# Gate and down weights on SyncE's queue behind the last token transpose, up weights on ScalarE's: a linear-attention and GEGLU block on one core

## The chip, the cores and the metric

The kernel runs on one core of a Trainium2 chip. The core has five engines that work side by side, each through its own list of instructions in order: TensorE (matmuls, PE in the profile), VectorE (DVE), ScalarE (ACT), GpSimd (POOL) and SyncE (SP), which here only issues DMAs. DMAs are issued on a queue of SyncE's or of ScalarE's, and the packets of both queues are moved by the same 16 DMA engines. The metric is the device time of one execution in microseconds (us); less is better.

## The reference

The block has two halves, both on x of 2048 tokens by 448 features, in bf16:

```python
h  = x + A(layernorm(x))          # linear attention, 16 heads of 28
h2 = h + B(layernorm(h))          # gated MLP, 448 -> 1792 -> 448

# A: q, k, v = split(x @ wqkv); phi(t) = where(t > 0, t + 1, exp(t)) + 1e-6
kv  = einsum("bhsd,bhse->bhde", phi(k), v)      # a sum over all tokens
z   = einsum("bhsd->bhd", phi(k))               # a sum over all tokens
o   = einsum("bhqd,bhde->bhqe", phi(q), kv) / (einsum("bhqd,bhd->bhq", phi(q), z) + 1e-6)
A   = o @ wo
# B:
B   = (gelu(x @ w_gate) * (x @ w_up)) @ w_down
```

So no token's attention output can be made before all tokens' keys have gone into kv and z. The gate and up weights are 448 x 1792 each (1.6 MB), the down weights 1792 x 448 (1.6 MB).

## The kernel before

The 2048 tokens are 16 tiles of 128. The work has three stages.

*Keys and queries.* For each tile, VectorE, ScalarE and GpSimd normalise the tokens (`ln_tile`, lines 430 to 455). The first four tiles are transposed by TensorE, the other twelve by DMA transposes on SyncE's queue (xT_4 to xT_15, line 455). TensorE then multiplies by the key or query weights (k_t and q_t, line 469), and adds phi(k) times the normalised tokens into four PSUM banks over all tiles (pt, line 488). ScalarE and VectorE make phi.

*The turn.* When the last key tile is in, kv is formed (line 527), masked by heads (kvm, line 531), and multiplied by wo into w2 (lines 547 to 553). Two DMAs on SyncE's queue, dws0 and dws1 (line 555), copy w2 into w2s with the two halves of the partitions exchanged. From here on the tiles go in pairs (`a2_pair`, line 558): the normalised queries of pair p are transposed, for pair 0 by TensorE (tro, line 599), for the others by a DMA on SyncE's queue (oT_1 to oT_7, line 605). The attention output of pair 0 is out1 (line 617), that of the other pairs is outA_p and outB_p (lines 627 and 628), which use pqnT, w2 and w2s and run two matmuls at once on the two halves of TensorE's rows. hr adds the residual (line 633), then come the second layernorm and its transposes: trh_0 and trh_1 on TensorE for pair 0 (line 654), and DMA transposes hT_2 to hT_15 on SyncE's queue (line 665), each behind a copy wrap_t on VectorE (line 664).

*The MLP.* The tokens go in chunks of 2, 2, 4, 4 and 4 tiles (`gu_chunk`, line 707). gu2_v and gu4_v (lines 726 and 728) multiply by gate weights on rows 0 to 63 and by up weights on rows 64 to 127 at the same time, so the gate weights lie in partitions 0 to 63 of wgu_sb and the up weights in partitions 64 to 127. ScalarE applies the GELU (ge, line 746) and VectorE the product (hm, line 748). downA_p and downB_p (line 696) multiply by wd_sb, fo adds the residual (line 702), and do_t stores the tile (line 703; the last two tiles, lines 678 to 683).

*The order.* Every task is numbered as it is created, and ORDERS (line 15) gives for each engine the full list of task numbers in the order in which it is to run them, in the order TensorE, ScalarE, VectorE, GpSimd, SyncE. `place` (line 130) checks that the lists agree with the dependencies, and `plan` (line 174) works out the semaphore waits. HOLD (line 51) says which of several waits of one task is put first. An engine that waits for one task holds up all that follows in its list. DMAs made by `dma` (line 345) keep their order of creation on a queue, through `last`.

The weights of the MLP are five loads: dwg0 and dwu0 (the first 768 of the 1792 columns of gate and up, 672 KB each), dwg1 and dwu1 (the other 1024, 896 KB each) and dwd (down, 1568 KB, 128 partitions). Before, the four gate and up loads stand on ScalarE's queue in the order dwg0, dwu0, dwg1, dwu1, created at lines 510 and 511 to run no earlier than ek_11, the exponential of key tile 11. dwd stands on ScalarE's queue too, created at line 609 with pair 1, and runs behind ge1_0, the first GELUs.

The order of the engines around the turn, before, by task names:

```text
SyncE:   ... xT_14 xT_15 dws0 dws1 oT_1 oT_2 oT_3 hT_2 hT_3 oT_4 hT_5 hT_4 hT_6 hT_7 oT_5 ...
ScalarE: ... ek_12 ek_13 dwg0 ek_14 dwu0 rq_4 ek_15 dwg1 eq_4 z1 eq_5 rq_5 dwu1 deA_0 ...
         ... ge0_0 ge1_0 deP_3 dwd ge1_1 ge0_1 ...
TensorE: ... out1_0 out1_1 q_11 q_12 q_13 q_15 q_14 outA_1 trh_0 trh_1 outB_1 gu2_0 gu2_1 outA_2
         gu2_2 outB_2 gu2_3 gu2_4 gu2_5 outA_3 gu2_6 outB_3 downA_0 gu2_7 gu2_8 downB_0 ...
```

Of the kernel before, what the change touches and what calls it, by code (L numbers as in the profile page):

```python
# [12 lines left out]


ORDERS = (
    "29 35 37 46 44 66 71 62 64 53 55 76 79 84 70 75 89 83 104 99 119 88 114 103 129 141 118 153 133 177 145 157"
    " 165 190 222 203 216 232 169 182 248 195 181 194 207 208 220 236 252 238 221 237 253 260 254 294 257 263 299"
    " 301 297 303 321 266 323 325 326 269 272 275 281 278 362 339 343 363 431 436 388 441 389 446 451 456 414 461"
    " 415 466 498 503 467 508 513 481 518 523 482 528 565 548 570 575 549 580 533 585 590 656 595 657 600 605 610"
    " 534 682 615 620 683 625 630 699 704 709 635 714 719 724 636 729 734 739 744 641 749 754 642 764 759 786 781"  # L20
    " 769 796 791 770 806 801 816 811 775 826 821 776 836 831 846 841 851 860 852 857 863",
    "3 5 6 7 28 32 33 41 42 36 59 60 45 50 51 67 54 72 63 94 77 95 80 109 110 78 124 85 125 136 137 91 90 148 172"
    " 149 100 173 185 106 186 115 105 160 130 161 142 211 243 198 199 154 120 212 244 178 227 121 228 166 191 204"
    " 217 284 233 285 224 249 286 223 288 239 240 287 314 292 291 261 256 262 318 353 259 357 255 302 298 322 324"
    " 258 268 264 265 271 270 267 333 335 334 336 277 384 283 279 282 276 340 274 273 280 345 432 434 410 361 439"
    " 437 444 442 449 447 452 454 457 459 462 477 464 501 499 506 504 544 509 511 516 514 519 521 524 526 529 531"
    " 568 566 571 573 652 578 581 576 583 678 586 588 593 591 598 596 601 603 613 608 611 606 616 618 623 621 628"
    " 626 631 633 700 702 712 707 705 710 715 717 720 725 727 722 730 732 737 735 747 745 742 740 757 750 752 755"
    " 767 765 760 762 787 784 782 789 794 797 799 792 807 809 802 804 812 817 814 819 822 829 824 827 839 837 834"
    " 832 849 847 842 844",  # L30
    "0 30 31 39 40 34 57 43 58 38 48 49 47 61 52 68 92 56 93 69 65 107 73 108 74 122 81 123 82 134 86 135 146 170"
    " 147 171 87 183 158 184 101 159 102 196 241 197 116 242 117 209 131 210 132 225 1 143 226 144 155 156 179 180"
    " 167 168 192 193 346 307 218 219 234 205 308 206 235 309 250 251 348 347 349 290 289 310 311 313 293 315 317"
    " 316 352 295 356 319 379 296 358 354 300 320 304 359 355 380 327 330 328 331 329 405 332 383 337 341 385 338"
    " 342 386 406 344 364 367 365 409 433 435 411 472 412 366 440 438 368 369 443 445 393 390 450 448 391 473 377"
    " 374 453 455 394 460 458 539 395 476 540 392 465 463 419 420 416 478 417 421 479 502 543 418 400 403 500 673"
    " 470 505 507 647 545 426 648 429 512 510 515 517 546 520 522 525 468 527 483 486 532 530 651 487 567 569 572"
    " 574 653 484 674 654 553 550 577 488 579 677 551 584 582 587 589 679 594 554 485 592 552 555 680 597 599 661"
    " 602 604 560 662 658 563 493 607 609 612 496 537 614 619 617 624 687 622 629 627 659 535 634 632 701 703 688"
    " 708 706 711 713 716 663 660 718 684 721 689 723 685 637 728 726 686 733 731 736 738 639 694 748 743 671 697"  # L40
    " 741 668 746 758 753 756 751 768 766 645 643 761 763 788 785 790 783 800 793 798 795 773 771 810 808 805 803"
    " 815 820 818 813 828 830 823 825 840 838 779 833 835 777 850 848 845 843 853 855 861 858 864",
    "15 16 27 19 22 21 17 96 97 111 25 112 126 127 138 139 150 151 26 23 174 162 187 175 200 188 163 245 201 18 213"
    " 214 229 20 230 24 246 312 350 351 381 382 407 408 370 371 372 373 376 474 475 397 541 398 396 542 402 399 422"
    " 423 424 425 428 649 650 676 675 490 491 489 557 558 556 492 562 559 495 664 665 691 666 692 667 690 693 696"
    " 670",
    "2 4 8 9 10 11 12 13 14 98 113 128 140 152 176 189 164 202 215 231 247 305 306 360 387 413 375 378 480 404 401"
    " 427 430 547 655 681 471 564 561 497 494 538 638 469 672 698 669 695 536 774 778 644 780 640 646 856 862 772"
    " 859 854 865",
)  # L50
HOLD = {
    32: (31,), 66: (36,), 99: (98,), 175: (174,), 188: (187,), 232: (231,), 294: (291,), 305: (298,), 362: (360,),
    388: (387,), 498: (378,), 767: (764,), 787: (786,), 807: (806,), 839: (836,), 864: (863,),
}


# [173 lines left out]
def bass_sequential_preLN__linear_attn_block__glu_gated_geglu__prompt_kernel(  # L230
# [19 lines left out]
    with es:  # L250
        block = es.enter_context(nc.Block())

        def sb(name, shape, dt):
            return es.enter_context(nc.sbuf_tensor(name, shape, dt))
# [7 lines left out]
        wgu_sb = sb("wgu_sb", [128, NK, FF], BF16)  # L262
        wd_sb = sb("wd_sb", [128, NJ, D], BF16)
# [41 lines left out]
        def bufs(name, n):  # L305
            return [_Buf("%s%d" % (name, i)) for i in range(n)]
# [7 lines left out]
        b_wo, b_wg, b_wu, b_wd = _Buf("wo"), bufs("wg", 2), bufs("wu", 2), _Buf("wd")  # L314
# [15 lines left out]
        A_, B_ = slice(0, 64), slice(64, 128)  # L330
# [14 lines left out]
        def dma(q, out_ap, in_ap, w, name, r=(), after=()):  # L345
            t_ = G.add(q, lambda e: e.dma_start(out_ap, in_ap), r=r, w=w, name=name, kind="dma", after=list(after) + last[q])
            last[q] = [t_]
            return t_

        def op(eng, fn, r, w, name, after=()):  # L350
            return G.add(eng, fn, r=r, w=w, name=name, after=after)
# [106 lines left out]
        eks = []  # L458
# [48 lines left out]
        xts = [t for t in G.all if t.name.startswith("xT_")]  # L507
        for i in range(2):
            cs = slice(0, FC) if i == 0 else slice(FC, FF)
            dma("act", wgu_sb[A_, :, cs], B_w_gate[:, cs].rearrange("(k p) n -> p k n", p=64), [b_wg[i]], "dwg%d" % i, after=eks[11:12])  # L510
            dma("act", wgu_sb[B_, :, cs], B_w_up[:, cs].rearrange("(k p) n -> p k n", p=64), [b_wu[i]], "dwu%d" % i, after=eks[11:12])


        op("act", lambda e: e.activation(zbc[B_, :], ps[B_, BK_PT[3], 0:D], AF.Identity), [b_ps[BK_PT[3]]], [b_z[1]], "z1")
        op("dve", lambda e: e.tensor_copy(zbc[A_, :], zbc[B_, :]), [b_z[1]], [b_z[0]], "z0")
# [42 lines left out]
        def a2_pair(p):  # L558
# [3 lines left out]
            if p < 2:  # L562
# [3 lines left out]
                for t in (a, a + 1):  # L566
                    n = t % 2
                    eng = "dve" if t in T1_DVE else "pool"
                    op(eng, lambda e, t=t, n=n: e.tensor_tensor(t1[:, n, :], pq[:, t, :], zbc[:, :], ALU.mult), [b_pq[t]] + b_z, [b_t1[n]], "t1%s_%d" % (eng[0], t))
                for t in (a, a + 1):  # L570
                    n, i = t % 2, t % 4
# [8 lines left out]
            else:  # L580
                i, b2 = 2 * (p % 2), slice(a, a + 2)
# [22 lines left out]
            else:  # L604
                G.add("sp", lambda e, i2=i2: e.dma_start_transpose(pqnT[:, i2, 0:NK, :], pqn[:, i2, 0:2 * D]),
                      r=b_pqn[i2], w=b_pqnT[i2], name="oT_%d" % p, kind="dma")

            if p == 1:
                dma("act", wd_sb[:, :, :], B_w_down.rearrange("(j p) n -> p j n", p=128), [b_wd], "dwd")

            if p == 0:
                for n in range(2):
# [139 lines left out]
        for nt in B1_CHUNKS:  # L752
            while done < min(P, (t0 + HR) // 2):
                a2_pair(done)
                done += 1
                if tbl2 is None:
                    tbl2 = G.add("act", lambda e: e.preload_act_table(AF.Gelu_apprx_tanh), name="tbl2", kind="nosync", after=exps)
            gu_chunk(t0, nt)
            for t in range(t0, t0 + nt, 2):
                if t < T - 2:  # L760
                    b2_pair(t // 2)
                else:
                    b2_tile(t)
                    b2_tile(t + 1)
            t0 += nt
# [52 lines left out]
```

## Time and profile before

| what | us |
|---|---|
| median of 3 runs | 191.95 |
| range of the runs | 191.61 to 192.84 |
| the profiled execution, its own time | 192.45 |
| its span, from the first to the last instruction | 190.7 |
| TensorE busy | 185.5 |
| VectorE busy | 127.7 |
| ScalarE busy | 76.0 |
| GpSimd busy | 52.3 |

The granted TensorE clock was 0.999. All times in the text below that name a place ("at 49.35") are microseconds from the start of the profiled span. The profile is one execution; the runs were timed without it. TensorE's busy time counts a stretch once, even if two matmuls run in it at the same time; the matmuls' ends are modelled, so the distance between the starts of two matmuls tells more of TensorE's speed than the length of one. A task of the kernel is found in the profile by its line, its engine and its place in the engine's order.

In a row of the profile, "L627 <- DMA pqnT<-pqn" reads: an instruction of line 627 waited for the DMA that writes the tile pqnT from the tile pqn. "SPq" and "ACTq" are the instructions of SyncE and ScalarE that issue DMAs; the time behind them is that of the issue, and the DMA lands later.

### The profile page before, as it was taken

To read this page: it belongs to the slowest core of one execution; us is meant where nothing else is said; L and a number is where in the kernel's file an instruction comes from. 1 tells how busy PE (TensorE), PEld (TensorE's weight loads), DVE (VectorE), ACT (ScalarE), POOL (GpSimd) and SP (SyncE) were. 2 spreads that over 40 slices of the span, in tenths; PEclk is the share of its full clock that TensorE was granted. 3 is DMA by queue.
4 is the path that set the end of the run, shared out by engine and by line. 5 is a ranking of instruction groups with operands and counts; after the bars stand their busy time and mean duration, and the time that the engine had idled before them with its cause. 6 is when DMAs were issued, how large, how long until landed. Compare 5 with 4: busy or idle time off the path is not lost.

```text
span 190.7 us, 4456 instructions
## 1 busy us (share of the span) xinstructions
PE 185.5 (97%) x1813; PEld 113.6 (60%) x1813; DVE 127.7 (67%) x328; ACT 76.0 (40%) x220; POOL 52.3 (27%) x91
## 2 busy tenths in 40 slices
PE   7999999999899999999999999999999999999994
PEld 7654455465488676977866675554554554554643
DVE  3999968999899997888885674446436234225232
ACT  3777656589874312342323143222223122224100
POOL 5078550524405596402348000007200000000000
PEclk9999999999999999999999999999999999999999
DMA  5986546999429507820204640001291000000303
GB/s 174 378 222 64 111 97 142 217 214 214 74 49 339 100 3 144 96 53 3 48 3 72 123 97 2 0 3 48 49 129 44 3 0 24 3 0 0 124 0 120
DMA packets 35076, 17.11 MB, mean 90 GB/s; under 512 B 26864, under 2 KB 33648, under 8 KB 35056
## 3 DMA queue, kind: packets, MB, share of 16 engines
q1 hardware_dynamic: 30688, 11.44, 30.0%
q10 hardware_dynamic: 4368, 5.39, 12.0%
q8 instruction: 14, 0.23, 0.5%
q14 instruction: 6, 0.05, 0.1%
HBM read 8.26 MB, written 1.84 MB: 53 GB/s over the span
## 4 chain that ended last, share of the span: by engine, by line
PE 79%; DVE 10%; DMA 9%; ACT 1%; issue 0%
PE ps L728 29%; PE ps L696 19%; PE ps L726 13%; DMA pqnT<-pqn 6%; PE ps L469 5%; PE ps L488 4%; DVE st L413 3%; PE ps L627 3%; PE ps L678 3%; DMA xnT<-xnn 2%; PE ps L628 2%; DMA x_sb<-in_A_x_dram 1%; DVE pk L482 1%; DVE pqn L576 1%; DVE mv L414 1%; DVE w L553 1%
## 5 line engine op out<-in xcount | busy, mean ns | idle before, releaser
L728 PE MATMUL ps<-hnT,wgu_sb 64*128 64x512 bf16 (+1 forms) x490 | 88.9, 333 | 0.0
L726 PE MATMUL ps<-hnT,wgu_sb 64*128 64x512 bf16 (+1 forms) x490 | 88.6, 333 | 0.0
L748 DVE TENSOR_TENSOR hh<-ps,gl 128x256 bf16<-128x256 f32 x112 | 42.5, 416 | 41.0 <-ACT gl L746 40.3
L746 ACT ACTIVATE gl<-ps 128x256 bf16<-128x256 f32 x112 | 36.2, 383 | 84.3 <-PE ps L726 84.3
L728 PEld LDWEIGHTS ps<-hnT,wgu_sb 64*128 64x128 bf16 x490 | 45.1, 94 | 26.7 <-DVE hh L748 3.1
L726 PEld LDWEIGHTS ps<-hnT,wgu_sb 64*128 64x128 bf16 x490 | 45.4, 94 | 5.1 <-DVE hnT L660 0.5
L696 PE MATMUL ps<-wd_sb,hh 64*128 64x448 bf16 x392 | 41.5, 349 | 0.0
L696 PEld LDWEIGHTS ps<-wd_sb,hh 64*128 64x128 bf16 x392 | 23.3, 94 | 14.2 <-issue 0.2
L469 PE MATMUL ps<-wqk_sb,xnT 128*128 128x448 bf16 x128 | 26.9, 353 | 0.4 <-DMA xnT<-xnn 0.4
L413 DVE BATCH_NORM_STATS2 st<-x_sb 128x6 f32<-128x448 bf16 x32 | 19.3, 612 | 2.0 <-DMA x_sb<-in_A_x_dram 1.9
L469 PEld LDWEIGHTS ps<-wqk_sb,xnT 128*128 128x128 bf16 x128 | 12.1, 98 | 12.0 <-ACT ln L420 0.7
L585 POOL TENSOR_TENSOR t<-pq,zbc 128x448 f32<-128x448 bf16 x12 | 13.2, 1117 | 22.0 <-DVE pq L583 22.0
L702 DVE TENSOR_TENSOR x_sb<-ps,x_sb 128x448 bf16<-128x448 f32 x14 | 8.4, 617 | 8.3 <-PE ps L696 8.3
L488 PE MATMUL ps<-pk,xnn 128*128 128x448 bf16 x64 | 13.7, 352 | 0.0
L417 POOL TENSOR_SCALAR nm<-mv 128x1 f32<-128x1 f32 (+1 forms) x19 | 4.3, 228 | 32.3 <-DVE mv L414 31.9
L627 PE MATMUL ps<-w,pqnT 64*128 64x448 bf16 x49 | 11.5, 350 | 1.0 <-DMA pqnT<-pqn 1.0
L662 POOL TENSOR_SCALAR hn<-x_sb,nm,rs 128x448 bf16<-128x448 bf16 x14 | 11.0, 792 | 0.3
L480 ACT ACTIVATE e<-ps 128x448 bf16<-128x448 f32 x16 | 8.7, 542 | 5.9 <-PE ps L469 5.8
L628 PE MATMUL ps<-pt_sb,pqnT 64*128 64x448 bf16 x42 | 10.2, 350 | 0.0
L453 POOL TENSOR_SCALAR xnn<-x_sb,nm,rs 128x448 bf16<-128x448 bf16 x12 | 9.0, 747 | 4.0 <-ACT rs L422 3.8
L482 DVE SCALAR_TENSOR_TENSOR pk<-ps,e 128x448 bf16<-128x448 f32 x16 | 9.8, 619 | 0.2
L488 PEld LDWEIGHTS ps<-pk,xnn 128*128 128x128 bf16 x64 | 6.3, 98 | 5.8 <-DVE pk L482 0.2
(83 smaller groups left out, 156.7 us busy)
## 6 DMA issues: line engine op xcount, KB each, us to landing
out_dram<-x_sb SPq DMA_DIRECT2D x15, 112.0 KB, 1.8
wd_sb<-in_B_w_down_dram ACTq DMA_DIRECT2D x1, 1568.0 KB, 7.2
x_sb<-in_A_x_dram SPq DMA_DIRECT2D x3, 448.0 KB, 6.6
wgu_sb<-in_B_w_gate_dram ACTq DMA_DIRECT2D x1, 896.0 KB, 10.8
wgu_sb<-in_B_w_up_dram ACTq DMA_DIRECT2D x1, 896.0 KB, 12.8
wgu_sb<-in_B_w_gate_dram ACTq DMA_DIRECT2D x1, 672.0 KB, 6.2
wgu_sb<-in_B_w_up_dram ACTq DMA_DIRECT2D x1, 672.0 KB, 8.6
wo_sb<-in_A_wo_dram SPq DMA_DIRECT2D x1, 392.0 KB, 8.1
```

The lines of the kernel that those rows point to most:

```text
L413: op("dve", lambda e: e.bn_stats(st[:, t, :], src_ap), [b_src], [b_st[t]], "bnst%s_%d" % (tag, t))
L469: ins = e.matmul(ps[:, bk, 0:D], xnT[:, t, k, :], wqk_sb[:, k, c0:c0 + D], start=(k == 0), stop=(k == 3))
L482: op("dve", lambda e: e.scalar_tensor_tensor(pk[:, ip, :], psK, EPS, e1[:, i, :], ALU.max, ALU.add), [b_ps[bk], b_e1[i]], [b_pk[ip]], "pk_ ...
L488: ins = e.matmul(ps[:, BK_PT[c], 0:D], xnn[:, t % XN_R, c * 128:(c + 1) * 128], pk[:, ip, :], start=(t == 0), stop=(t == T - 1))
L585: op("pool", lambda e, n=n: e.tensor_tensor(t1[:, n, :], pq[:, a + n, :], zbc[:, :], ALU.mult), [b_pq[a + n]] + b_z, [b_t1[n]], "t1p_%d" % ...
L627: e.matmul(ps[:, BK_OUT[0], 0:D], pqnT[ra, i2, sg // 2, :], w2[ra, sg // 2, :], start=(sg == 0), stop=(sg == 5))
L628: ins = e.matmul(ps[:, BK_OUT[1], 0:D], pqnT[rb, i2, 3 + (sg + 1) // 2, :], (w2 if sg == 6 else w2s)[rb, sg // 2, :], start=(sg == 0), sto ...
L696: ins = e.matmul(ps[:, BK_O[n], 0:D], hh[rows, j, sl[n]], wd_sb[rows, j, :], start=(half == 0 and j == 0), stop=(half == 1 and j == NJ - 1))
L726: first = e.matmul(psG[:, jj * N:(jj + 1) * N], wgu_sb[A_, k, j * 128:(j + 1) * 128], hnT[A_, ka_, c0:c0 + N], start=(k == 0), stop=(k == ...
L728: ins = e.matmul(psU[:, jj * N:(jj + 1) * N], wgu_sb[B_, k, j * 128:(j + 1) * 128], hnT[B_, kb_, c0:c0 + N], start=(k == 0), stop=(k == NK ...
L746: G.add("act", lambda e, gi=gi, cs_=cs_, psG=psG: e.activation(gl[:, gi, cs_], psG[:, cs_], AF.Gelu_apprx_tanh), r=[b_ps[BK_G[i]]], w=[b_g ...
L748: op("dve", lambda e, dst=dst, srcU=srcU, srcL=srcL: e.tensor_tensor(dst, srcU, srcL, ALU.mult), [b_ps[BK_U[i]], b_glh], [b_ar[j_][t % HR] ...
```

## The change

The four loads of gate and up are split over the two queues, and the down load is moved with them. dwg0, dwg1 and dwd are issued by SyncE directly behind the last token transpose, in this order; dwu0 and dwu1 by ScalarE behind ek_14, one after the other. dws0, dws1 and all later DMAs of SyncE's queue stand behind dwd. No load changes its size or its place in memory.

```diff
         for i in range(2):
             cs = slice(0, FC) if i == 0 else slice(FC, FF)
-            dma("act", wgu_sb[A_, :, cs], B_w_gate[:, cs].rearrange("(k p) n -> p k n", p=64), [b_wg[i]], "dwg%d" % i, after=eks[11:12])
-            dma("act", wgu_sb[B_, :, cs], B_w_up[:, cs].rearrange("(k p) n -> p k n", p=64), [b_wu[i]], "dwu%d" % i, after=eks[11:12])
-
+            dma("sp", wgu_sb[A_, :, cs], B_w_gate[:, cs].rearrange("(k p) n -> p k n", p=64), [b_wg[i]], "dwg%d" % i, after=xts[-1:])
+            dma("act", wgu_sb[B_, :, cs], B_w_up[:, cs].rearrange("(k p) n -> p k n", p=64), [b_wu[i]], "dwu%d" % i, after=eks[13:14])
+
+
+        dma("sp", wd_sb[:, :, :], B_w_down.rearrange("(j p) n -> p j n", p=128), [b_wd], "dwd", after=xts[-1:])
...
-            if p == 1:
-                dma("act", wd_sb[:, :, :], B_w_down.rearrange("(j p) n -> p j n", p=128), [b_wd], "dwd")
```

ORDERS and HOLD are written anew, for all five engines. No other instruction is added or taken away. By task names, the new orders read, around the turn:

```text
SyncE:   ... xT_12 xT_15 xT_14 dwg0 dwg1 dwd dws0 dws1 oT_1 oT_2 oT_3 hT_3 hT_2 oT_4 oT_5
         hT_7 hT_6 hT_4 hT_5 oT_6 do_1 oT_7 ...
ScalarE: ... ek_11 ek_13 ek_12 ek_15 ek_14 dwu0 dwu1 z1 eq_4 rq_4 evpA_1 deA_0 ...
         ... ge1_0 ge0_0 ge1_1 ge0_1 deP_3 ...
TensorE: ... out1_1 out1_0 q_10 q_13 q_15 q_12 outA_1 trh_0 trh_1 q_14 outB_1 gu2_0 gu2_1 outA_2
         gu2_2 outB_2 gu2_3 gu2_4 gu2_5 outA_3 gu2_6 outB_3 downA_0 gu2_7 gu2_8 downB_0 outA_4 gu2_9
         outB_4 gu2_10 gu2_11 gu2_12 outA_5 gu2_13 outB_5 downA_1 gu4_15 gu4_14 downB_1 ...
VectorE: ... aqP_3 pnP_2 evhD_1 ... hm0_1 pnP_3 hm0_2 ... hm0_9 hr_8 wrap_7 hm0_10 hm1_10
         wrap_6 wrap_5 wrap_4 ...
```

At the end, SyncE's order of the stores becomes do_10 do_7 do_8 do_0 do_9 do_15 do_13 do_12 do_2 do_6 do_11 do_14 do_15; before it was do_7 do_13 do_15 do_8 do_14 do_12 do_15. GpSimd's order is changed within the same stages. In the key stage, TensorE takes k_9 ahead of k_10, k_13 ahead of k_12, and k_15 ahead of k_14, and q_4 behind the last keys.

## Prediction

> **What bounds the kernel now.** I read the page's table of engines first, then the waits, the chain that ended last, the issues and landings of the DMAs, and last the stretches by window, where a stage's own limit shows.
>
> TensorE is the bound nearly everywhere:
>
> ```profile
> PE 185.5 (97%) x1813; PEld 113.6 (60%) x1813; DVE 127.7 (67%) x328; ACT 76.0 (40%) x220; POOL 52.3 (27%) x91
> ```
>
> Little can be won: 190.7 - 185.5 = 5.2 us of the span is without a matmul, and part of that is the start and the last store. The waits of TensorE's weight loads on a DMA name the place near the change (total, times, longest), and the chain shows the two transposes behind it (start, length):
>
> ```profile
> PEld ps L627 <- DMA pqnT<-pqn: 1.8, 2, 1.3
> ```
>
> ```profile
> 43.78 5.53 DMA pqnT<-pqn
> 49.35 0.36 PE ps L627
> ...
> 57.05 5.73 DMA pqnT<-pqn
> 62.83 0.36 PE ps L627
> ```
>
> The first row is oT_1, after which outA_1 starts at 49.35; the second is oT_3, before outA_3. Both take about twice their usual time (the list of DMA issues: KB, us to landing):
>
> ```profile
> wd_sb<-in_B_w_down_dram ACTq DMA_DIRECT2D x1, 1568.0 KB, 7.2
> pt_sb<-w SPq DMA_DIRECT2D x2, 168.0 KB, 5.7
> pqnT<-pqn SPq DMA_TRANSPOSE x7, 2.9
> ```
>
> Who was in the way is seen in the timeline, with the end of the token transposes (11.19 + 17.12 = 28.31), the first gate load, the last up load, the two copies of w (dws0, dws1) and the down load:
>
> ```profile
> 11.19 17.12 SPq L455 DMA_TRANSPOSE xnT<-xnn  x12
> 42.37 1.13 SPq L346 DMA_DIRECT2D pt_sb<-w  x2
> ```
>
> ```profile
> 29.02 0.66 ACTq L346 DMA_DIRECT2D wgu_sb<-in_B_w_gate_dram  x1
> 34.88 0.60 ACTq L346 DMA_DIRECT2D wgu_sb<-in_B_w_up_dram  x1
> 54.60 0.39 ACTq L346 DMA_DIRECT2D wd_sb<-in_B_w_down_dram  x1
> ```
>
> and in the windows (last two columns: busy share of the 16 DMA engines, GB/s):
>
> ```profile
> 31.00:34.00 3.00, 3.00 (x18) 1.55 (x16) 2.97 (x9) 1.09 (x2) 0.00 (x0) 1.00 1.02 225
> 37.00:41.00 4.00, 4.00 (x34) 2.30 (x33) 3.93 (x13) 3.81 (x11) 2.39 (x3) 1.00 1.08 216
> 44.00:46.00 2.00, 2.00 (x12) 1.07 (x11) 2.00 (x5) 1.97 (x6) 1.64 (x2) 1.00 1.05 208
> 46.00:47.00 1.00, 1.00 (x7) 0.49 (x5) 1.00 (x5) 1.00 (x5) 0.40 (x1) 1.00 1.02 225
> 57.00:60.00 3.00, 3.00 (x55) 2.60 (x53) 2.97 (x10) 1.12 (x4) 1.16 (x3) 1.00 1.06 369
> ```
>
> The reader is to see three things. From 31 to 46 the DMA engines are full (share over 1.0) with gate and up weights, at only about 215 GB/s: each of these loads fills 64 partitions. The down load, over 128 partitions, runs at 369. And dws0/dws1, issued at 42.37, moved nearly nothing, by the packets of SyncE's queue, until the weights had drained at about 45.5; then came 0.34 MB at about 225 (1.5 us), and behind them oT_1. So TensorE's 1.0 us of idling before 49.35 is set by the end of the weight stream, though nobody needs gate and up before gu2_0 at 51.89, nor down before downA_0 at 65.7.
>
> **The change part by part.** *The down load, moved from 54.60 on ScalarE's queue to the front of dws0, dws1 and oT_1 on SyncE's.* The same 4.8 MB now has to leave before outA_1 can start. The stream starts behind the last token transpose, at 28.31 in place of 29.02: -0.7 us. It carries 1568 KB = 1.61 MB more: at 369 GB/s, +4.35 us. Gate, up and the rest are the same bytes; as long as the engines stay full, it matters little whose turn is first, since SyncE's queue holds two thirds of the bytes and drains last. So dws0 starts at 45.5 - 0.7 + 4.35 = 49.15, and outA_1 at 49.35 + 3.65 = 53.0.
>
> The open price is that of gate and up side by side: gate fills the lower 64 partitions, up the upper, and before they shared one queue, so they never ran together but for seams. Bounds: no gain from it (215 GB/s), or the rate of 128 partitions (369). The nearest row is 44 to 46, where dws0, to the lower half, starts while the last up load, to the upper half, still drains: 208 GB/s, no more than up alone. I take no gain, and keep 369 as the other end, since that seam is short. The Trainium skill bears on this, on its page "SBUF — State Buffer", section "Can I just issue two DMAs to hit both halves?": no, two concurrent DMAs to partition 0 and partition 64 gained 6% there over one. By that rule the 2.52 MB of half-width loads left when up joins would take about 11.1 instead of 11.7 us, and the sum would be 0.6 lower; the trace's seam agrees.
>
> *TensorE behind it.* outA_1 blocks all that follows in TensorE's order, gu2_0 included, which needs nothing from it. TensorE gets there at about 47.6 (48.35, the end of q_14 by the spacing of its matmuls, less q_14 itself, which now stands behind the transposes), so it idles some 5.4 us. Then come outA_1 (four pairs at 0.187: 0.75), trh_0 and trh_1 (50.22 to 51.10: 0.88), q_14 (0.76), outB_1 (0.57): gu2_0 at 53.0 + 2.96 = 55.96, for 51.89: **+4.07 us**. q_14 and outB_1 cover the evictions of trh, which had cost 0.2 to 0.35 us.
>
> *oT_3 free of the down load.* Its 5.73 falls to about the 2.9 of its kind; it is issued behind pnP_3, which follows gu2_1 on VectorE, some 7 us ahead of outA_3. The 0.35 us idled before 62.83 goes: **-0.35**.
>
> *Issues.* SyncE gets three of about 0.6 us in its idle stretch 28.3 to 42.4; behind them in its order stand only dws0 on, which wait for evwA_0 at 42.3 anyway. ScalarE loses dwg0, dwg1 and dwd, where it waited for TensorE; dwu0 and dwu1 now stand behind ek_14 (about 31), with z1 and eq_4 behind them, and 16 us before gu2_0 they are no matter: 0. Should that cover fail, 0.6 us each.
>
> *The new orders up to outA_1.* Waits of 0.43 (at 5.6), 0.35 (16.5) and 0.42 us (19.1) lie there. Bounds: all won (-1.2), or as much lost. With 5.4 us of room before outA_1 neither reaches the end: 0. Only the last token transpose counts, through the stream's start; SyncE issues them 1.3 us apart, and a different one last shifts it by some 0.7 either way: 0 taken. HOLD only sorts waits: 0.
>
> *The new orders after it.* Between 62.8 and 179.6 no gap between matmuls is above 0.06 us beyond streaming, so nothing can be won and something lost. The tightest: wrap_4 to wrap_6 now stand behind hm1_10 on VectorE, so hT_5 is issued about 30.5 us after gu2_0 starts and lands 3.1 later, at 33.6; gu4_15 needs it at 34.7 (before, the matching transpose landed 2.4 us early). It holds: 0, with a loss of up to 1 kept. In the tail five stores of 0.45 us are issued between the two halves of do_15; they end at about 188.4, and the last half is ready at 188.7: 0, up to +0.3.
>
> **Sum:** +4.07 - 0.35 = +3.72 on a span of 190.7: 194.4. The profiled execution took 192.45 for that span, so 196.2; the median of the runs, 191.95, is 0.5 below it. On that scale: **195.7 us**.
>
> **The rivals.** *A, halves side by side (not slower).* If gate and up overlap at full width, 0.69 MB goes alone from 30.0 to 33.2 and the other 4.13 MB at 369 until 44.4. dws0 starts 1.1 us earlier than before, outA_1 at 48.25, gu2_0 at 51.2: -0.7, with -0.35 behind it, -1.0: 190.9. It decides where the mixed rate of gate and up passes about 317, at which SyncE's queue drains at 45.5, as before (33.2 + 2.52 / 0.317 + 4.35). For it: each load alone reaches a little over half of 369. Against: the seam's 208. *A', in part:* at 290 GB/s the drain is at 46.2, gu2_0 about 1.2 late, less 0.35: 192.8.
>
> *B, still worse.* The SyncE queue restarts late or its issues stall behind so long a backlog (oT_1's issue took 1.66 us against a median of 1.26 in line 605), and the 1 us before gu4_15 is eaten: +1 to +2, 196.7 to 197.7.
>
> *C, the early waits are also won.* Needs A, and the 1.2 us as well, since outA_1 can't be before oT_1's own 2.9 us: about 189.7.
>
> *D, nothing moves:* the stream is hidden anyway. That needs dws0 to overtake what stands ahead of it on its queue; it did not between 43 and 45.
>
> **How the numbers follow.** Chances: forecast 0.62 (its own range 194.7 to 196.6, from 0.5 if the halves run at the 225 of two of the windows, 0.7 of the start, 0.3 of the tail), B 0.10, A' 0.11, A 0.10, C 0.05, D 0.02. A measurement of this kernel tells about 1% from no change. Over 1% faster, below 190.0, is C: 0.05. Within 1%, up to 193.9: A, A' and D: 0.23. Slower: 0.72. The range 191.8 to 197.8 leaves out A and C below and a little of B above.
>
> **What would show it.** The DMA share stays over 1.0 from about 30 to 51 at about 215 GB/s while gate and up run, near 370 only when down is alone; oT_1 takes about 9 us from issue to landing; outA_1 starts near 53 after an idle stretch of over 4 us; gu2_0 near 56; no wait at outA_3; no gap from there to the tail. I am wrong if the windows show 300 GB/s or more with both queues at work, or if dws0 moves bytes before down has drained.

## The result, and the profile after

| | before | after |
|---|---|---|
| median, us (6 runs each, on one chip) | 191.79 | 199.62 |
| range of the runs, us | 191.45 to 192.84 | 199.04 to 200.51 |
| ratio after to before, with 95% interval | | 1.0398 [1.0374, 1.0423] |
| profiled execution, own time and span, us | 192.45, 190.7 | 199.04, 197.3 |
| granted TensorE clock of the profiled execution | 0.999 | 0.991 |
| outA_1 starts, us | 49.35 | 54.21 |
| gu2_0 starts, us | 51.89 | 58.65 |

The changed kernel is 4.0% slower. The prediction had the sign, and 195.7 us, with 197.8 at the end of its range. All times below that name a place are again microseconds of a profiled span; line numbers behind the loads are one less than before (outA_1 is line 626).

The page of the changed kernel: the line of the engines, and from its 40 slices (4.9 us each) the granted clock.

```profile
PE 186.7 (95%) x1813; PEld 113.5 (58%) x1813; DVE 129.6 (66%) x328; ACT 76.9 (39%) x220; POOL 52.5 (27%) x91
...
PEclk9999999999979999999999999999999999999999
```

TensorE is busy 1.2 us longer with the same 1813 matmuls, and one slice, from 54.3 to 59.2, has a clock of 0.7. In the waits of the changed kernel (total, times, longest) the rows for pqnT are larger by far than before:

```profile
PEld ps L626 <- DMA pqnT<-pqn: 6.3, 1, 6.3
PE ps L626 <- DMA pqnT<-pqn: 5.9, 1, 5.9
```

They are the first weight load and the first matmul of outA_1. Each stands there once; the wait ahead of outA_3 has gone. The chain of waits of the changed kernel shows what is behind the transpose (start, length):

```profile
43.94 10.23 DMA pqnT<-pqn
...
54.21 0.55 PE ps L626
...
54.77 0.37 PE ps L626
...
55.14 0.37 PE ps L626
...
55.52 0.36 PE ps L626
...
55.89 1.49 PE ps L653 x14
57.38 0.76 PE ps L469 x4
58.13 0.29 PE ps L626
...
58.43 0.19 PE ps L626
```

oT_1 takes 10.23 us, where it took 5.53. The four pairs of outA_1 are 0.37 apart; the last pairs, of outB_1, are 0.19 apart, which is the spacing that the prediction used. trh_0 and trh_1 take 1.49 instead of 0.88; q_14, at 57.38, is back at 0.76. The list of DMA issues of the changed kernel (KB, median us to landing), and SyncE's timeline (start, length of the issue):

```profile
wd_sb<-in_B_w_down_dram SPq DMA_DIRECT2D x1, 1568.0 KB, 22.7
wgu_sb<-in_B_w_up_dram ACTq DMA_DIRECT2D x1, 896.0 KB, 17.7
pt_sb<-w SPq DMA_DIRECT2D x2, 168.0 KB, 10.3
```

```profile
28.45 1.33 SPq L346 DMA_DIRECT2D wgu_sb<-in_B_w_gate_dram  x2
29.82 0.62 SPq L346 DMA_DIRECT2D wd_sb<-in_B_w_down_dram  x1
42.49 1.40 SPq L346 DMA_DIRECT2D pt_sb<-w  x2
```

dws0 and dws1 are issued when they were before (42.49 for 42.37) and take 10.3 us in place of 5.7. The windows of the changed kernel show why, and where the clock falls (stretch, length, busy time of TensorE, weight loads, VectorE, ScalarE and GpSimd, then the granted clock, the share of the DMA engines, GB/s):

```profile
34.00:37.00 3.00, 3.00 (x17) 1.53 (x16) 2.90 (x7) 2.27 (x6) 2.02 (x2) 1.00 1.06 213
42.00:47.00 5.00, 5.00 (x33) 2.62 (x31) 4.87 (x11) 4.45 (x11) 2.04 (x2) 1.00 1.08 251
48.00:49.00 1.00, 0.30 (x2) 0.00 (x0) 1.00 (x5) 1.00 (x4) 0.00 (x0) 1.00 1.09 364
50.00:51.00 1.00, 0.00 (x0) 0.00 (x0) 0.70 (x1) 0.00 (x0) 1.00 (x1) 1.00 1.06 207
51.00:53.00 2.00, 0.00 (x0) 0.00 (x0) 0.00 (x0) 0.00 (x0) 1.59 (x2) 1.00 1.37 63
53.00:54.00 1.00, 0.00 (x0) 0.00 (x0) 0.00 (x0) 0.00 (x0) 0.00 (x0) 0.85 1.13 252
54.00:57.00 3.00, 2.79 (x20) 1.62 (x21) 0.00 (x0) 0.21 (x1) 0.00 (x0) 0.50 0.11 25
```

By the packets in the trace, gate runs alone from 29.9 to 37.9: up, issued at 30.98 and 31.67, moves its first byte at 37.5. So but for the last 0.4 us the two never ran side by side. From then to 47 up and down take turns, packet by packet, at 251 GB/s; then down is alone at 364. The first packet of dws0 leaves at 49.25, the last of the down load ends at 51.58, the last of dws at 52.78. From 51 to 53 the engines count as full but move 63 GB/s: 20 of oT_1's packets of 256 B are held there, for 1.0 to 2.0 us each, until 53.1.

Where the 6.6 us of span went: outA_1 4.86 later (54.21 - 49.35); from outA_1 to gu2_0 4.44 for 2.54, 1.90 more (0.42 of it was forecast, most of that for q_14, which now stands there); from gu2_0 to the end 138.61 for 138.78, 0.17 less. The sum is 6.59, from 190.67 to 197.26.

### The profile page after: what moved, and what is told of

Its sections match the earlier page's. It is cut to its first block, busy times and chain, and to the rows that moved or that the text cites. A ratio compares the mean times of both kernels' runs of the same rounds, so it can differ in the third digit from the quotient of the medians.

```text
span 197.3 us, 4458 instructions
## 1 busy us (share of the span) xinstructions
PE 186.7 (95%) x1813; PEld 113.5 (58%) x1813; DVE 129.6 (66%) x328; ACT 76.9 (39%) x220; POOL 52.5 (27%) x91
## 4 chain that ended last, share of the span: by engine, by line
PE 77%; DVE 12%; DMA 5%; POOL 2%; issue 1%; ACT 1%; POOLq 0%
PE ps L727 34%; PE ps L695 15%; PE ps L469 8%; DMA pqnT<-pqn 5%; PE ps L725 5%; PE ps L488 4%; PE ps L677 3%; PE ps L626 2%; PE ps L407 2%; DVE hh L747 2%; DVE st L413 2%; PE ps L627 1%; POOL hn L661 1%; DVE pk L482 1%; DVE den L588 1%
## 5 line engine op out<-in xcount | busy, mean ns | idle before, releaser
L727 PEld LDWEIGHTS ps<-hnT,wgu_sb 64*128 64x128 bf16 x490 | 45.3, 94 | 29.9 <-DVE hh L747 3.3
L725 PEld LDWEIGHTS ps<-hnT,wgu_sb 64*128 64x128 bf16 x490 | 45.5, 94 | 3.2
L469 PE MATMUL ps<-wqk_sb,xnT 128*128 128x448 bf16 x128 | 27.5, 353 | 0.5 <-ACT xnT L448 0.5
L626 PE MATMUL ps<-w,pqnT 64*128 64x448 bf16 x49 | 12.3, 367 | 5.9 <-DMA pqnT<-pqn 5.9
L701 DVE TENSOR_TENSOR x_sb<-ps,x_sb 128x448 bf16<-128x448 f32 x14 | 8.4, 618 | 10.0 <-PE ps L695 10.0
L425 POOL TENSOR_SCALAR ln<-mv 128x2 f32<-128x2 f32 x7 | 2.3, 331 | 41.2 <-DVE mv L414 41.0
L627 PE MATMUL ps<-pt_sb,pqnT 64*128 64x448 bf16 x42 | 10.8, 365 | 0.0
L661 POOL TENSOR_SCALAR hn<-x_sb,nm,rs 128x448 bf16<-128x448 bf16 x14 | 10.3, 742 | 0.3
L632 DVE TENSOR_TENSOR x_sb<-ps,x_sb 128x448 bf16<-128x448 f32 x16 | 9.7, 613 | 0.9 <-PE ps L627 0.8
```

The costliest lines, as they stand in the source:

```text
L469: ins = e.matmul(ps[:, bk, 0:D], xnT[:, t, k, :], wqk_sb[:, k, c0:c0 + D], start=(k == 0), stop=(k == 3))
L626: e.matmul(ps[:, BK_OUT[0], 0:D], pqnT[ra, i2, sg // 2, :], w2[ra, sg // 2, :], start=(sg == 0), stop=(sg == 5))
L627: ins = e.matmul(ps[:, BK_OUT[1], 0:D], pqnT[rb, i2, 3 + (sg + 1) // 2, :], (w2 if sg == 6 else w2s)[rb, sg // 2, :], start=(sg == 0), sto ...
L661: op("pool", lambda e, t=t, sh=sh: e.tensor_scalar(hn[:, sh, 0:D], x_sb[:, t, :], nm2[:, t:t + 1], rs2[:, t:t + 1], ALU.add, ALU.mult), [b ...
L725: first = e.matmul(psG[:, jj * N:(jj + 1) * N], wgu_sb[A_, k, j * 128:(j + 1) * 128], hnT[A_, ka_, c0:c0 + N], start=(k == 0), stop=(k == ...
L727: ins = e.matmul(psU[:, jj * N:(jj + 1) * N], wgu_sb[B_, k, j * 128:(j + 1) * 128], hnT[B_, kb_, c0:c0 + N], start=(k == 0), stop=(k == NK ...
```

## The experiments

The theory was: the place of the down load, ahead of dws0 and oT_1, is the whole loss; TensorE's idling while it drains then also costs clock. Against it stood: the new orders cost something of their own; the queue, not the bytes, holds oT_1 (SyncE's queue is served in order); and halves side by side would have saved the change. Ratios are to the before kernel in runs on the same chip as the experiment, where its median was 192.56 to 192.69; the change's 1.0398 is that of the table of the result. "Base" is the kernel that was edited.

| run | base | ratio [95%] | outA_1 at | matmuls' wait ahead of it; half clock |
|---|---|---|---|---|
| e1_loads_alone | before | 1.0342 [1.0299, 1.0385] | 54.87 | 5.53; 53.5 to 60.4 |
| e3_down_behind_oT1 | after | 1.0020 [0.9996, 1.0043] | 49.02 | 0.90; none |
| e12_half_down | after | 1.0122 [1.0068, 1.0177] | 51.71 | 2.92; none |
| e10_down_on_act | after | 1.0382 [1.0331, 1.0433] | 54.67 | 6.11; 52.9 to 59.7 |
| e4_filler | after | 1.0321 [1.0266, 1.0375] | 55.52 | 1.65, the rest filled; none (by the spacing of the matmuls) |
| e11_wide_filler | after | 1.0274 [1.0230, 1.0319] | 54.05 | filled; none |
| e2_orders_alone | before | 1.0327 [1.0284, 1.0370] | 54.72 | 4.11 ahead of a key tile; 35.4 to 38.8 |
| e5_orders_alone_late | before | 1.0164 [1.0111, 1.0218] | 51.16 | 2.42; 52.5 to 56.0 |
| e6_mlp_first | after | 1.0152 [1.0098, 1.0206] | 54.34 | 0.64 at trh_0 and at gu2_0, 1.34 at outA_2; none |
| e7_side_by_side | e3 | 1.0016 [0.9991, 1.0042] | 48.47 | 0.2, and 0.94 at outA_2; none |
| e8_before_trh_first | before | 1.0019 [0.9994, 1.0044] | 50.15 | 1.21 at gu2_0; none |
| e9_before_side_by_side | before | 0.9964 [0.9939, 0.9990] | 48.80 | none; none |

**The loads or the orders?** e1 has the old orders and the change's five loads:

```diff
 SyncE:   ... xT_14 xT_15
+         dwg0 dwg1 dwd
          dws0 dws1 oT_1 ...
 ScalarE: ... ek_13 ek_14 ek_15
+         dwu0 dwu1     (dwg0 dwu0 dwg1 dwu1 dwd leave their old places)
```

> The five loads as in the change (gate and down on SyncE's queue behind xT_15, up on ScalarE's behind ek_15), all other orders as before. Theory: the loss comes from the loads, of which the down load stands ahead of dws0, dws1 and oT_1; outA_1 starts at 53.5 to 54.5 in place of 49.35, TensorE idles over 5 us, its granted clock falls to half for some 3.4 us behind that, and the time is 198 to 200. Rival, the orders: half of the loss or more is missing here, 194 to 196.

It came out as the loads alone would have it, 3.4% slower, where the whole change is 4.0% slower; the two intervals overlap, so the remaining 0.6% is not told from noise. e1's timeline of TensorE (start, length, then in brackets the idle time before it and what ended it):

```profile
54.87 0.55 PE L640 MATMUL ps<-w,pqnT 64*128 64x448 bf16 x1 [5.53 <-DMA pqnT<-pqn]
```

e3 is the reverse: the changed kernel with only the down load moved back behind oT_1, on SyncE's queue.

```diff
 SyncE:   ... xT_15 xT_14 dwg0 dwg1
-         dwd dws0 dws1 oT_1
+         dws0 dws1 oT_1 dwd
          oT_2 ...
```

> The changed kernel with the down load alone moved, on SyncE's queue, from ahead of dws0 to behind oT_1; gate stays on SyncE's, up on ScalarE's queue. Theory: the 4.35 us of the down load no longer stand before outA_1; gate and up have drained at about 45, outA_1 starts at 48.3 to 49.3, the clock stays up, 191 to 193. Rival, the split of gate and up over two queues costs by itself: outA_1 at 51 or later, 194 or more.

Here is outA_1's first weight load in e3's timeline of the weight loads:

```profile
49.02 0.09 PEld L641 LDWEIGHTS ps<-w,pqnT 64*128 64x128 bf16 x1 [1.33 <-DMA pqnT<-pqn]
```

The transpose lands 0.3 us earlier than before the change (49.02 for 49.35), and the loss is gone: ratio 1.0020 with all the new orders in place. The place of the down load is shown to be the cause, and the new orders together with the split of gate and up cost nothing that can be measured (the interval reaches 0.4%, or 0.8 us).

e12 gives the dose: the down load cut in two, parts 0 to 6 where the change has them, 7 to 13 behind oT_1.

```diff
-dma("sp", wd_sb[:, :, :], B_w_down.rearrange("(j p) n -> p j n", p=128), [b_wd], "dwd", after=xts[-1:])
+wdv = B_w_down.rearrange("(j p) n -> p j n", p=128)
+dma("sp", wd_sb[:, 0:7, :], wdv[:, 0:7, :], [b_wd], "dwd", after=xts[-1:])
...
+dma("sp", wd_sb[:, 7:14, :], wdv[:, 7:14, :], [b_wd2], "dwe")   # behind oT_1
```

> The changed kernel with the down load cut in two: the first seven of its 14 parts stay ahead of dws0, the other seven go behind oT_1. Theory: the delay of outA_1 goes by the bytes ahead, so half of them costs about half: outA_1 at 51 to 52, an idle stretch of about 3.5 us, the time 194.5 to 197. Rival: the place on the queue costs by itself, and outA_1 stays over 53.

```profile
51.71 0.36 PE L643 MATMUL ps<-w,pqnT 64*128 64x448 bf16 x1 [2.92 <-DMA pqnT<-pqn]
```

This row of e12's timeline stands 2.36 us behind before's 49.35: half the bytes, 0.49 of the 4.86 us. And after 2.92 us of idling the clock stayed full in this profiled run; of the other three runs, one (196.64 us) had a mean clock of 0.991.

**The queue or the bytes?** e10 moves the down load from SyncE's queue to the end of ScalarE's, so that nothing but gate is ahead of dws0 on its own queue.

```diff
 SyncE:   ... xT_14 dwg0 dwg1
-         dwd
          dws0 dws1 oT_1 ...
 ScalarE: ... ek_14 dwu0 dwu1
+         dwd
          z1 eq_4 ...
```

> The changed kernel with the down load on ScalarE's queue behind dwu1, so that SyncE's queue has only gate ahead of dws0 and oT_1. If a later DMA waits for what the 16 engines already hold, whichever queue it came by: outA_1 at 49.5 to 51.5, the time 193.5 to 196. If only its own queue counts: outA_1 at 48 to 48.5, 191.5 to 193. If all bytes issued earlier have to leave first, as the prediction had it: outA_1 at 53 to 54.5, 198 to 200.

```profile
54.67 0.55 PE L639 MATMUL ps<-w,pqnT 64*128 64x448 bf16 x1 [6.11 <-DMA pqnT<-pqn]
```

By this row of e10's timeline, the other queue gains nothing for outA_1: the third case came, a little above its bounds (54.67, and 200.28 us). It came by another road, though. The first dws packet leaves at 47.75, 1.5 us earlier than in the change and long before the down load ends (54.16), but then the packets of oT_1 lie between those of the down load, from 49.65 to about 54. So a transpose is held by the bytes that are already handed to the 16 engines, on either queue.

**What the clock costs.** e4 and e11 put extra matmuls into an idle bank ahead of outA_1, which overwrites what they leave there; the work of the kernel is whole.

```diff
+def ffill(e):                                   # e4: 95 times 128 columns; e11:
+    ...
+    for _ in range(29):
+        ins = e.matmul(ps[:, BK_OUT[0], 0:D], ident[:], wqk_sb[:, 0, D:2 * D], start=True, stop=True)
+    ...
 TensorE: ... q_12
+    fill
     outA_1 trh_0 trh_1 q_14 ...
```

> The changed kernel with 95 extra matmuls of 128 columns on bank 5 between q_12 and outA_1, whose result is overwritten: some 5.2 us of TensorE work in a stretch where it idles 5.9. Theory: outA_1 still starts at 54.2, since its transpose sets that, but the clock stays at full, so gu2_0 starts at about 57.2 in place of 58.65, and the time falls by 1.5 to 2.5 us, to 197 to 198. Rival, the clock costs nothing that is not hidden: within 0.5 of 199.6.

The matmuls of outA_1 stood 0.19 apart, as at full clock, and gu2_0 followed outA_1 by 3.09 us for 4.44. But outA_1 itself came at 55.52: on one DMA engine an instruction fetch of 16 KB, from 53.43 to 54.48, stands directly behind the transpose's packets, and of the sixteen parts of its landing one came at 53.99 and fifteen at 55.31 to 55.48; e11, which has no fetch there, has all of them by 54.00. The time, 198.88 us, missed its forecast. So it says little of the clock's price, and e11 makes the same stretch of work with a third of the instructions:

> The clock again, as e4_filler, in which the 95 extra instructions pulled a 16 KB instruction fetch into the transposes and oT_1 landed 1.3 us later: now 29 matmuls of 448 columns, some 5.4 us of TensorE work, on bank 5 ahead of outA_1, the result overwritten. Theory: outA_1 at 54.2 to 54.9, granted clock full behind it, gu2_0 2.9 to 3.1 after outA_1 in place of 4.4, the time 197 to 198.5. Rival, the clock costs nothing: 199 to 200.

The windows of e11, to be set beside the row 54 to 57 above:

```profile
54.00:57.00 3.00, 2.98 (x33) 1.67 (x34) 0.62 (x1) 1.49 (x3) 0.00 (x0) 1.00 0.08 15
```

outA_1 starts at 54.05, as in the change, but with a clock of 1.00, and 33 matmuls fit where 20 did; gu2_0 follows 3.08 us later. The ratio falls from 1.0398 to 1.0274, so the clock is worth about 1.2%, or 2.4 us (0.16 of that is outA_1's earlier start). The profiled run lost 1.48 (4.44 - 2.96) in a short drop: a clock of 0.991 over 197.3 us is about 3.5 us at half. Four of the six runs of the change had 0.983, about 6.7 us at half, and were 0.9 us slower in the mean (200.03 for 199.13); with two thirds of 0.9, that is 2.1.

**The orders alone.** e2 has the new orders, with the loads on ScalarE's queue as near to their old places as those orders allow; e5 has all four gate and up loads behind ek_14 there.

```diff
 ScalarE: ... ek_11 ek_13
+         dwg0               (e2; dwu0 behind ek_12, dwg1 behind ek_14, dwu1 behind rq_4)
          ek_12 ek_15 ek_14
+         dwg0 dwu0 dwg1 dwu1   (e5)
          z1 ... ge1_0 ge0_0
+         dwd                (e2 and e5)
```

> The new orders on all engines, the five loads on ScalarE's queue at their old places (dwg0 behind ek_13, dwu0 behind ek_12, dwg1 behind ek_14, dwu1 behind rq_4, dwd behind ge0_0). Theory: outA_1 within 0.5 us of 49.35, no drop of the clock behind it, 191.5 to 193. Rival, the orders: 194 or more, with gaps at 39 (0.7 us in the changed kernel) and at gu4_14 (0.3 us).

This missed the theory's numbers (outA_1 at 54.72, 198.83 us). The trace puts the loss not on the orders of the engines but on where they let the first weight load go. Two issues and one matmul from e2's timeline:

```profile
27.75 1.19 SPq L468 DMA_TRANSPOSE xnT<-xnn  x1
27.92 0.69 ACTq L359 DMA_DIRECT2D wgu_sb<-in_B_w_gate_dram  x1
...
34.82 1.13 PE L482 MATMUL ps<-wqk_sb,xnT 128*128 128x448 bf16 x4 [4.11 <-DMA xnT<-xnn]
```

The first weight load is issued 0.2 us after the last token transpose, whose data then lands some 7 us later, and a key tile waits 4.11 us, with half the clock from 35.4 to 38.8. It looks like the change's loss at another transpose. e5 takes that away:

> The new orders, with all four gate and up loads on ScalarE's queue behind ek_14 (dwg0 dwu0 dwg1 dwu1, so behind the landing of the last token transpose) and dwd behind ge0_0; this mends e2_orders_alone, in which dwg0 was issued 0.2 us behind xT_14 and the transpose landed some 7 us late. Theory: the orders by themselves cost little. The loads start at about 31 in place of 29.0, drain at about 47.5, so outA_1 is at about 51 and the time 193 to 195, all of it from the later start. Rival, the orders: the time is over 196, with gaps that do not follow a transpose.

e5 starts its stream at about 31, 2 us later than before, and outA_1 comes 1.8 us later. Its median, 195.63, is above the forecast, between theory and rival. Two of its four runs had a clock of 1.000 (194.87 and 195.02 us) and two 0.991 (196.24 and 196.32): 1.34 us for one drop, in one kernel. At full clock it is 2.3 us over the kernel before (194.95 - 192.69), 1.8 of them outA_1's; the other 0.5 stays open. So e2 and e5 don't clear the orders to the last half microsecond; e3 is the cleaner answer. The profiled run of e5 is one of those with a drop, and its TensorE idled for less time than e12's (the row names VectorE, but the weight load beside it waits 2.9 us for the DMA of pqnT):

```profile
51.16 0.36 PE L641 MATMUL ps<-w,pqnT 64*128 64x448 bf16 x1 [2.42 <-DVE pqn L604]
```

Its clock falls to half at 52.54, 1.4 us after this matmul, and stays there until 55.95.

**Where the idle time could have gone.** e6 gives TensorE other work ahead of outA_1, on the changed kernel; e8 does the like on the kernel before, whose TensorE idles about 1 us there.

```diff
 TensorE (e6): ... q_12
+         trh_0 trh_1 q_14 gu2_0 gu2_1
          outA_1 outB_1 outA_2 ...            (hm1_0 hm0_0 hm1_1 hm0_1 ahead of hr_3 on VectorE)
 TensorE (e8): ... q_15 q_14
+         trh_0 trh_1
          outA_1 outB_1 gu2_0 ...             (dwd behind oT_1 on SyncE)
```

> The changed kernel, its loads untouched, with trh_0, trh_1, q_14, gu2_0 and gu2_1 moved ahead of outA_1 on TensorE, and hm of gu2_0 and gu2_1 ahead of hr_3 on VectorE. Theory: outA_1 is late by the transposes alone, and 4.5 us of work that doesn't need them was queued behind it; with that work in the idle stretch the clock stays up, outA_2 starts at 56 to 57 in place of 61.7, and the time is 193 to 195. Rival, something behind the turn is the loss: over 197.

> A version that might beat both: the kernel before, with the down load alone moved, to SyncE's queue behind oT_1, and trh_0 and trh_1 ahead of outA_1 (with drP_2, rdP_2, deP_2 and evhA_0 shifted to fit). gu2_0 at about 51.0 in place of 51.9 and no wait at outA_3 (0.35): 190.5 to 191.5 where the kernel before has 192. Rival: TensorE finds the next wait, within 0.3 of the kernel before.

e6 wins back the larger part (1.0152 for 1.0398; its 195.28 us are just above the forecast): outA_1 is no earlier, but TensorE works in the meantime and the clock stays full. A rest stays: it idles 0.64 us each ahead of trh_0 and gu2_0, whose inputs are not ready so soon, and outA_2, at 57.41, waits 1.34 us for the residual of pair 1 on VectorE. e8 wins nothing, as its rival had it; the wait has only moved to gu2_0, which now needs the eviction of transposes that have just run, by this row of its timeline (gu2_0 started at 51.89 before):

```profile
53.10 0.28 PE L740 MATMUL ps<-hnT,wgu_sb 64*128 64x256 bf16 x1 [1.21 <-DVE hnT L674]
```

**Halves side by side.** e7 is e3 with dwg0 held until ek_15, so that gate and up are issued together, at 30.8 to 31.7. e9 is the kernel before with all four loads together behind ek_12, gate on SyncE's queue and up on ScalarE's, and the down load behind oT_2.

```diff
 # e7, on e3
-dma("sp", wgu_sb[A_, :, cs], ..., "dwg%d" % i, after=xts[-1:])
+dma("sp", wgu_sb[A_, :, cs], ..., "dwg%d" % i, after=xts[-1:], sync=eks[15:16])
 # e9, on the kernel before
-dma("act", wgu_sb[A_, :, cs], ..., "dwg%d" % i, after=eks[11:12])
-dma("act", wgu_sb[B_, :, cs], ..., "dwu%d" % i, after=eks[11:12])
+dma("sp", wgu_sb[A_, :, cs], ..., "dwg%d" % i, after=xts[-1:], sync=eks[12:13])
+dma("act", wgu_sb[B_, :, cs], ..., "dwu%d" % i, after=eks[12:13])
```

> As e3_down_behind_oT1, but dwg0 waits for ek_15, so gate on SyncE's queue and up on ScalarE's are issued together at about 31; in the changed kernel up moved its first byte when gate had drained, so the two never ran together. If halves gain nothing from running together (215 GB/s, as the prediction took it): drained at 46.5 to 47.5, outA_1 at 50.5 to 51.5, 193.5 to 195. If they add up (369): drained at 41, dws0 and oT_1 free, outA_1 at about 48, 190.5 to 192.

> A version that might beat both, from what e7_side_by_side showed: the orders of the kernel before, gate on SyncE's queue and up on ScalarE's, all four issued together behind ek_12 at about 29, and down on SyncE's queue behind oT_2. If the halves add up as there (380 GB/s where both run): drained by 43, outA_1 at about 48.4 in place of 49.35, no wait at outA_3, 190.8 to 191.8 where the kernel before has 192.5. Rival: the side-by-side stretch is too short, or the next wait takes its place, and the time is within 0.3 of the kernel before.

The windows of e7 and then of e9:

```profile
36.00:37.00 1.00, 1.00 (x8) 0.49 (x6) 1.00 (x3) 1.00 (x4) 1.00 (x2) 1.00 1.10 243
39.00:43.00 4.00, 3.49 (x24) 1.70 (x23) 4.00 (x12) 3.46 (x9) 0.00 (x0) 1.00 1.05 373
```

```profile
33.00:35.00 2.00, 2.00 (x12) 1.05 (x11) 1.97 (x6) 0.56 (x2) 0.00 (x0) 1.00 1.10 224
37.00:40.00 3.00, 2.86 (x27) 1.70 (x26) 2.92 (x8) 2.84 (x8) 2.74 (x3) 1.00 1.05 378
```

In both, the first gate load and the first up load still go for the most part one after the other (243 and 224 GB/s); the second ones, when both queues have packets waiting, run side by side at 373 and 378. The Trainium skill, on its page "SBUF — State Buffer", section "Can I just issue two DMAs to hit both halves?", gives two such DMAs 6% over one; here they move 1.5 to 1.7 times the rate of the row before, so the measurement decides against it. In e9 the stream has drained at 41.6, dws0 and dws1 land 2.7 us behind their issue, and TensorE waits for no pqnT. Its ratio of 0.9964 has an interval that ends below 1: it beats the kernel before by 0.4%, though its 191.97 us fall just short of the forecast. How much of this is due to the halves and how much to the moved down load was not separated. e7 gains nothing over e3 and misses its forecast (192.79 us): its down load stands between oT_1 and oT_2, and outA_2 waits 0.94 for oT_2.

## Why the prediction was right and wrong

*The stream behind oT_1: the right mechanism, mis-sized.* The term was +3.65 for outA_1; it measured +4.86. dws0 was to start at 49.15, and its first packet leaves at 49.25. But the old start, which I read as 45.5, was 45.07 by the packets, so the shift is 4.18. The tail from the first dws packet to the last grew too, from 2.93 us (45.07 to 48.00) to 3.53 (49.25 to 52.78): the mean drain of the engines was as forecast, but the slowest engine ended the down load only at 51.58, and oT_1's packets were held until 53.1. From the last dws packet to outA_1 it is 1.35 and 1.43 us. So 4.18 + 0.60 + 0.08 = 4.86: 0.53 of the missing 1.21 is my reading of the start, 0.6 the slowest engine. No run tests why it lags, but the packets point at an instruction fetch: one of 16 KB runs on one engine from 42.26 to 43.51, and after it one engine is behind. A load is closed by 16 packets of 4 B, as many as there are DMA engines; fifteen of those of dwu1 end by 47.45, one at 48.59. In e12 the fetch (42.63 to 43.89) falls on the end of dwu0, and there fifteen end by 42.70 and one at 43.90, just behind the fetch. The kernel before has such a fetch too (43.58 to 44.93), where the last of the sixteen ends at 46.84 and the one ahead of it at 46.19, so the fetch is not the change's doing.

The prediction's second sign, dws0 moving bytes before down has drained, did show to the letter (49.25 for 51.58), but not for the reason behind it. By the packets dws0 did not overtake the down load on any engine: it began on those that had ended their part, and its last eight packets leave one after another from 51.58, when the last packet of the down load has ended.

*Side by side: the assumption was wrong as a statement of the chip, and by luck did no harm here.* I took no gain from the seam's 208 GB/s, a weak row: dws0's first packet left at 45.07, so the window from 44 to 46 has both for less than 1 us. e7 and e9 show 373 and 378. But the change doesn't get it, since up's first byte came only when gate had drained. So rival A did not come, and the sign named for it, 300 GB/s with both queues at work, did not show: 251 while up ran beside down.

*"TensorE behind it": the step that failed.* I timed outA_1, trh, q_14 and outB_1 by rows at full clock, 2.96 us up to gu2_0; they took 4.44. After the idle stretch the granted clock was 0.50 from about 53.7 to 57.1, and the four pairs of outA_1 went from 0.187 to 0.37 apart. The prediction had seen 5.4 us of idling and used it only as cover for other delays; it left out that idling has a price. e11, which fills the stretch, gives back 1.2%. The Trainium skill has the rule, on its page "TensorE: Matmul & The Clock Gate", section "HAM oscillation — how this bites in real kernels": no idle gap of TensorE above about 3.4 us, or the next work starts at half clock. The trace agrees that the change's idling of 5.91 us is followed by half clock, but not with the bound: e5 shows a drop after 2.42 us. By that rule the forecast 5.4 us of idling had a price; with a drop as long as the trace's 3.4 us it is 1.7 us, an estimate, and 197.4 would have been the forecast.

*oT_3: right.* The 0.35 us are gone; outA_3 starts at 69.14 without a wait.

*Issues and orders: nearly right.* Waits of 0.74, 0.24 and 0.68 us (at 5.6, 24.5 and 39.2) lie ahead of outA_1 and were swallowed, as said. hT_5 was in time for gu4_15. The tail is unchanged: 2.39 us for 2.40. Not foreseen is a gap of 0.32 us at 86.3, where the gate and up matmuls (line 727) wait for VectorE's product (line 747) to free a bank; with it, the part behind gu2_0 is 0.18 us over the -0.35 that I gave it.

*The sum.* Missed are 1.21 (the stream's drain), 1.48 (clock) and 0.18: 2.87 us, from 3.72 to 6.59. That is the span's difference. The median missed by 3.92 (199.62 - 195.7), since the profiled run of before was 0.5 over its median and that of the change is 0.58 under its own, four of whose six runs have the longer drops.

*The range.* Its upper end was made of a slow queue and of the lost slack at gu4_15. Both rest on rows in which TensorE is never idle for long, so no row could show the clock; the term was missing, not narrow.

## What to carry to other kernels

A load that nobody needs soon belongs behind the last small transfer that the critical engine waits for, on whichever queue: "as early as possible" puts its bytes ahead of that transfer. If a change makes TensorE idle for some 2.4 us or more, reckon that 3.4 to 6.8 us of the work behind may run at half clock, or give it work there. Loads to opposite halves of the partitions are worth issuing together on two queues, so that both have packets waiting.

## What the runs showed of the hardware

- A DMA that is issued on an idle queue can wait for what the engines hold from the other: up moved its first byte 6.5 us after its issue (30.98 to 37.5). After that the two queues take turns, packet by packet: between 38 and 47, 854 packets of down leave and 837 of up.
- Two loads to opposite halves run at 373 to 378 GB/s when both are waiting, against 213 to 243 for one.
- A DMA transpose behind weights is late far beyond its own time: 10.23 us for oT_1, and some 7 us in e2 behind a load issued 0.2 us after it. In e4 an instruction fetch of 16 KB on one engine (53.43 to 54.48) came directly behind the packets of oT_1, and most of its landing came 1.5 us later than in e11, which has no such fetch.
- The held packets of a transpose are let go together, a little behind the last packet of the slowest engine; this is seen in the traces, not tested. In the change the 20 held packets of oT_1 all end at 53.12 to 53.15, 0.35 us behind the last dws packet (52.78). Before it was 48.34 to 48.38 for 48.00, in e3 47.89 to 47.93 for 47.55, in e12 50.61 to 50.64 for 50.27. In e9, where the weights had drained 2.3 us before dws0 began, no packet of oT_1 took over 0.1 us.
- The drops of the clock came in two lengths, 3.4 us (the change, e2, e5) and 6.8 us (e1, e10), and not from one length of idling: in the profiled runs after 2.42 us in e5, 4.11 in e2 and 5.91 in the change, but not after 2.92 in e12 or about 1 before. They began 3.8 (e5) to 5.4 us (the change) after the idling did, so that in e2 and e5 the matmuls had been back at work for 0.6 and 1.4 us. What decides between 2.4 and 2.9 us of idling stays open.
